# Two groups of v products in a pair of heads instead of three, and the side work placed anew

## The chip, the cores and the metric

The kernel runs on one core of a Trainium2 chip. The metric is the device time of one execution in microseconds (us). A core has five engines that run on their own and meet at semaphores: TensorE (PE) for matmuls, VectorE (DVE), ScalarE (ACT), GpSimd (POOL), and SyncE (SP), whose queue issues most transfers.

## The reference

```
# q, k, v: [4 batches, 8 heads, 768, 64]; centroids: [8 heads, 16, 64]
q_assign = argmax(normed(q) @ normed(centroids).T)        # the same for k
scores   = where(q_assign == k_assign, q @ k.T / 8, -1e9)
attn     = softmax(scores);  x = attn @ v                 # 3072 tokens of 512
skip     = x @ w_skip > 0;   e = argmax(x @ w_gate)       # 8 experts
out      = x + (skip ? gate * relu(x @ w1[e]) @ w2[e] : 0)
```

## The kernel before

Attention comes first, then the experts. Attention works on 16 pairs of heads, one after the other. Queries are taken in two halves of 384 (hf), keys in six tiles of 128 (kt), and the two heads of a pair are a = 0 and 1. So a pair has 24 score tiles, and `score(i, s)` makes one: two matmuls into one bank (the high parts with the mask rows and the maxima as extra rows, L652; the products of high and low parts, L653), `exp` on ScalarE (L655) into one of `NPT` buffers, and GpSimd's running sum of it (L661, L667). `smax` looks ahead for the next pair, 24 times per pair: one matmul of high parts, 128 queries by 384 keys (L603), whose row maxima VectorE takes (L605). `avs` multiplies finished exp tiles with v, in full fp32 and with the two heads in two column halves of the array (L678). It runs in groups of `GROUP` key tiles, both heads of each.

The order of everything is written out by hand. A time is a number of score steps from the pair's first score, 24 steps to a pair, and `steps` issues all steps of all pairs in the order of these times, each on its engine's queue, in order. `PLAN` holds the times of an ordinary pair, `FIRST`, `LAST` and `END` those of the first and last pairs. Negative times lie in earlier pairs: -46.48 is step 1.52 of the pair two before. So the work around a group at step 1.6, 9.6 or 17.6 belongs to several pairs:

- `sims` (L509): similarities of a later pair to the centroids, on TensorE; `assign` finds the nearest centroid on VectorE in seven operations; `masks` makes the mask rows on ScalarE (L566) and sends them in eight transfers (L572).
- `split_hi` (ScalarE, L450) and `split_lo` (VectorE, L460) split q and k; `copies_hi` and `copies_lo` are transfers on SP's queue.
- `mneg` (VectorE, L619) joins the maxima of one half; `mrows` turns them on TensorE (L627), and ScalarE copies them into the score operand (L638) in three pieces.
- `sums` (TensorE, L719) and `recip` (VectorE) make the softmax divisors; `av_out` (ScalarE, L704, L707) takes a group's result out of its bank.
- `xout` turns a half of the output (L780, three turns), scales it on VectorE (`scale_out`, L785) or on ScalarE (`scale_rows`, L802, six copies) and sends it.
- After each batch (four pairs), `route_a` (TensorE, L861), `route_gates` and `route_slots` choose experts, VectorE's steps at the times of `GATES` and `SLOTS`.

Score banks: eight PSUM banks are handed out in turn; a step takes two, one for the scores and one for the maxima.

```
    "av": 1.6, "oT": (0.35, 3.55), "sums": 33.55, ...
        for g in range(n, 2 * KT + 1, n):
            add(2 * g + p["av"], self.avs, keys[g - n:g])
```

With n = 4 the groups of a pair come at 9.6, 17.6 and 25.6, the last of these at step 1.6 of the next pair.

Of the kernel before, what the change touches and what calls it, by code (L numbers as in the profile page):

```python
# [13 lines left out]
F32 = mybir.dt.float32  # L14
# [9 lines left out]
P = 128  # L24
# [4 lines left out]
KT = S // P  # L29
# [19 lines left out]


PLAN = {
    "load": -60.0, "load_v": -45.0, "weights": 72.0, "sims": -46.48, "assign": (-46.42, 0.02, 0.02, 0.02, (-38.42,), 0.02),
    "hi": (-38.405, -38.40), "masks": (-32.5, 0.12), "lo": (-30.38, -22.38), "copies": (-22.1, -21.2, -21.1),
    "smax": (-21.6, 1.0, -0.2), "mneg": (-9.2, 4.0), "mrows": ((-6.5, 0.2, 0.05), (9.62, 0.1, 0.05)),
    "av": 1.6, "oT": (0.35, 3.55), "sums": 33.55, "recip": 33.56, "xout": (33.66, 49.55, 41.55),
    "route": (41.5, 41.55, 65.5), "early": (86.1, 100.9),
}

GATES = (41.62, 41.63, 41.64, 41.65, 41.66, 49.66, 49.67, 49.68, 49.69, 49.7, 57.5, 58.5,
         65.603, 65.604, 65.605, 65.606, 65.607, 65.608, 65.609, 65.61, 65.7)  # L60
SLOTS = ((73.69, 73.7, 73.71, 73.72, 89.65, 97.68, 97.69, 97.7, 97.71, 105.66, 113.66, 117.2, 117.4,
          121.66, 121.67, 121.68, 121.69, 121.7, 121.71, 121.72),
         (73.601, 73.602, 73.603, 73.604, 73.605, 73.606, 73.7, 81.651, 81.652, 81.655, 81.66, 85.0, 85.2,
          86.6, 86.61, 104.4, 104.41, 104.42, 104.43, 104.44))
FIRST = {
    0: {
        "load_v": -18.9, "sims": -20.0, "hi": (-19.9, -19.8, -19.7, -19.6), "assign": (-19.0, 0.1, 0.01, 0.01, 0.01, 0.01),
        "lo": (-18.7, -18.6, -16.9, -16.8), "masks": -17.0, "smax": (-14.0, 0.1, 14.1, 0.7), "mneg": (-12.85, 9.3),
        "mrows": ((-12.8, 0.1, 0.0), (9.65, 0.1, 0.0)),
    },  # L70
    1: {
        "sims": -42.2, "hi": (-42.4, -42.3), "lo": (-40.1, -40.0), "copies": (-20.9, -20.8, -20.7), "load_v": -14.0,
        "assign": (-36.83, 12.93, 0.2, 0.2, 0.2, 0.2), "masks": (-21.6, 0.1), "smax": (-15.6, 0.95, -0.1),
        "mneg": (-4.6, 6.6), "mrows": ((-3.8, 0.2, 0.05), (9.45, 0.1, 0.05)),
    },
    2: {
        "load": -62.0, "load_v": -37.0, "sims": -38.46, "assign": (-38.42, 0.02, 0.02, 0.02, (-30.38,), 0.02), "hi": (-36.2, -30.3), "lo": (-22.39, -22.38), "masks": (-26.0, 0.12), "smax": (-17.6, 0.97, 0.0), "mneg": (-6.4, 5.2),
    },
    3: {"load": -64.0},
    4: {"load": -63.5},  # L80
}

LAST = {"sums": 29.2, "recip": 29.21, "xout": (31.52, 49.55, 37.55)}
END = {"mrows": ((-6.3, 0.2, 0.05), (5.5, 0.1, 0.05)), "mneg": (-9.2, 1.45)}

GROUP = (4, 3)


class Kernel:
# [6 lines left out]
    def run(self):  # L96
        tc = self.tc
        with ExitStack() as ctx:
            self.const = ctx.enter_context(tc.tile_pool(name="const", bufs=1))
            self.raw = ctx.enter_context(tc.tile_pool(name="rawp", bufs=RING))  # L100
            self.halves, self.chosen, self.apart_rows = {}, {}, False

            self.both = ctx.enter_context(tc.tile_pool(name="both", bufs=1))
            self.D = self.both.tile([P, 66 * 256], F32R, name="D")
            self.NPT = 12
            self.PT = self.const.tile([P, self.NPT, HALF + 1], F32, name="PT")
            psum = ctx.enter_context(tc.tile_pool(name="psum", bufs=1, space=PSUM))
# [233 lines left out]
    def tasks(self, i):  # L341

        p, last = {**PLAN, **FIRST.get(i, {}), **({self.npair - 2: LAST, self.npair - 1: END}.get(i, {}))}, i == self.npair - 1
        r = [(s, lambda s=s: self.score(i, s)) for s in range(NS)]
        add = lambda t, f, *a: r.append((t, lambda: f(i, *a)))
        if i:
            add(p["load"], self.load)
        add(p["load_v"], self.load_v)
        if i == 2:
            for a in range(2):  # L350
                add(8.0 + 6.0 * a - i * NS, self.set_rows, a)
        add(p["sims"], self.sims)
# [836 lines left out]
    def ending(self, i):  # L1189

        j = [i // HP * KT + hf * NB for hf in range(2)]
# [13 lines left out]
        for t, c, k in ((25.8, 0, 0), (25.87, 0, 1), (25.94, 0, 2), (25.95, 0, 3), (25.96, 1, 0), (26.05, 1, 1),  # L1205
# [16 lines left out]
    def early_lists(self, i):  # L1222
# [4 lines left out]
        yield (86.3,)  # L1227
# [679 lines left out]
```

## Time and profile before

| | |
|---|---|
| Time, median of 3 runs | 595.55 us (594.94 to 595.74) |
| Profiled execution | 594.91 us, of which the span of the trace is 593.2 us |
| Granted TensorE clock, mean | 0.997 of full speed |

The span runs from the first to the last instruction. Start times in the rows are us from its start. In rows in order of time, the second number is how long the merged instructions lasted, and x is their count. Matmuls overlap: one that lasts 0.34 us may start 0.18 us after another, so starts are compared, not lengths.

### The profile page before, as it was taken

The page shows a single profiled execution, that of the slowest core. Times are in us where ns is not written, and L with a number is a line of the kernel's source. Part 1 is how long each engine was busy: PE and PEld are TensorE (multiplying, and loading weights), DVE is VectorE, ACT ScalarE, POOL GpSimd, SP SyncE. Part 2 cuts the span into 40 slices and gives each one's busy share as a digit, 9 for nine tenths or more (in the row PEclk, how much of TensorE's full clock was granted, in tenths as well). Part 3 has the DMA queues.
Part 4 walks back from the last instruction along what each step waited for, and adds up shares of the span by engine and source line. Part 5 has one row for each costly group of instructions (what it writes and reads, how often), then busy time and mean ns, then how long its engine had stood idle before and what let it go on. Part 6 is the DMA issues. An engine that isn't in the chain of part 4 may idle for free.

```text
span 593.2 us, 12894 instructions
## 1 busy us (share of the span) xinstructions
PE 581.6 (98%) x4225; PEld 419.3 (71%) x4225; DVE 500.6 (84%) x1070; ACT 390.8 (66%) x836; POOL 351.6 (59%) x389
## 2 busy tenths in 40 slices
PE   7999999999999999999999999999999999999996
PEld 3566677767777667776677767775589896677784
DVE  6989897789998989999999999998869863678783
ACT  7466777767777677676777668885336443666572
POOL 7797777867768778577777677784021251243111
PEclk9999999999999999999999999999999999999998
DMA  7378797696876857557576564232344595978860
GB/s 221 85 209 174 183 249 180 189 238 201 231 194 189 201 148 203 141 150 189 152 211 158 135 173 114 75 104 85 110 143 152 206 335 197 362 254 270 268 233 36
DMA packets 53813, 109.00 MB, mean 184 GB/s; under 512 B 8365, under 2 KB 22573, under 8 KB 53744
## 3 DMA queue, kind: packets, MB, share of 16 engines
q1 hardware_dynamic: 51232, 101.92, 60.4%
q0 software_dynamic: 2112, 6.03, 2.9%
q8 instruction: 35, 0.57, 0.4%
q14 instruction: 34, 0.28, 0.2%
q10 hardware_dynamic: 400, 0.20, 0.1%
HBM read 59.95 MB, written 9.57 MB: 117 GB/s over the span
## 4 chain that ended last, share of the span: by engine, by line
PE 86%; issue 5%; DVE 4%; ACT 2%; DMA 1%; POOL 1%; POOLq 0%; SPq 0%; ACTq 0%; DVEq 0%
PE ps L678 22%; PE ps L652 12%; PE ps L603 11%; PE ps L653 11%; PE ps L1095 5%; PE ps L1096 5%; PE ps L1097 5%; PE ps L780 2%; PE ps L719 2%; PE ps L509 2%; PE ps L1690 1%; PE ps L1665 1%; PE ps L627 1%; DMA D<-mk 1%; PE ps L1516 1%
## 5 line engine op out<-in xcount | busy, mean ns | idle before, releaser
L667 POOL TENSOR_TENSOR acc<-acc,PT 128x384 f32<-128x384 f32 x246 | 233.9, 981 | 50.9 <-ACT PT L655 50.7
L605 DVE TENSOR_REDUCE M<-ps 128x1 f32<-128x384 f32 x384 | 197.9, 553 | 16.2 <-PE ps L603 13.4
L655 ACT ACTIVATE PT<-ps 128x384 f32<-128x384 f32 x384 | 177.6, 491 | 35.5 <-PE ps L653 22.6
L652 PE MATMUL ps<-D 102*128 102x384 f32 x384 | 137.2, 357 | 0.0
L678 PE MATMUL ps<-PT,vt 128*64 128x385 f32 x768 | 135.1, 493 | 0.0
L603 PE MATMUL ps<-D 96*128 96x384 f32 x384 | 130.0, 345 | 2.1 <-ACT D L583 1.0
L653 PE MATMUL ps<-D 128*128 128x384 f32 x384 | 130.2, 339 | 0.0
L678 PEld LDWEIGHTS ps<-PT,vt 128*64 128x64 f32 x768 | 50.6, 136 | 61.3 <-issue 56.9
L652 PEld LDWEIGHTS ps<-D 102*128 102x128 f32 x384 | 72.8, 190 | 22.7 <-issue 7.2
L661 POOL TENSOR_TENSOR acc<-PT 128x384 f32<-128x384 f32 x64 | 54.5, 869 | 47.8 <-ACT PT L655 47.7
L603 PEld LDWEIGHTS ps<-D 96*128 96x128 f32 x384 | 73.0, 190 | 5.5 <-ACT D L583 1.4
L653 PEld LDWEIGHTS ps<-D 128*128 128x128 f32 x384 | 73.1, 190 | 0.0
L638 ACT ACTIVATE D<-ps,blocks 6x256 fp32r<-6x256 f32 x84 | 33.2, 456 | 28.0 <-PE ps L627 27.7
L1504 ACT ACTIVATE D<-wraw 128x1024 fp32r<-128x1024 f32 (+1 forms) x45 | 43.2, 997 | 1.4 <-PE ps L1097 1.0
L1509 DVE TENSOR_TENSOR D<-wraw,D 128x1024 fp32r<-128x1024 f32 (+1 forms) x29 | 33.6, 1183 | 6.0 <-ACT D L1504 6.0
L1272 POOL DMA_INDIRECT out<-yo,idws x9 | 11.8, 1314 | 45.2 <-DVE yo L1129 32.4
L460 DVE TENSOR_TENSOR raw<-raw,D 128x768 fp32r<-128x768 f32 x28 | 29.5, 1055 | 0.1
L1272 POOL DMA_INDIRECT out<-PT,idws x4 | 6.5, 1636 | 36.4 <-DVE PT L1701 24.4
L802 ACT ACTIVATE x<-ps,rs 128x64 f32<-128x64 f32 x84 | 18.7, 321 | 11.5 <-PE ps L780 11.5
L1095 PE MATMUL ps<-D 128*128 128x512 f32 x60 | 24.9, 414 | 0.0
L450 ACT ACTIVATE D<-raw 128x768 fp32r<-128x768 f32 x30 | 23.7, 835 | 0.8 <-issue 0.7
L704 ACT ACTIVATE vm<-ps 128x1 f32<-128x1 f32 x31 | 5.3, 172 | 26.1 <-PE ps L678 25.9
(352 smaller groups left out, 943.6 us busy)
## 6 DMA issues: line engine op xcount, KB each, us to landing
wraw<-w SPq DMA_DIRECT2D x72, 512.0 KB, 6.1
D<-D SPq DMA_DIRECT2D x124, 192.0 KB, 3.4
raw<-qk SPq DMA_DIRECT2D x16, 768.0 KB, 5.7
D<-raw SPq DMA_DIRECT2D x60, 192.0 KB, 3.5
vt<-v SPq DMA_DIRECT2D x16, 384.0 KB, 4.1
out<-x SPq DMA_DIRECT2D x31, 192.0 KB, 2.6
D<-mk SPq DMA_DIRECT2D x120, 24.0 KB, 2.0
out<-x ACTq DMA_DIRECT2D x1, 192.0 KB
```

The lines of the kernel that those rows point to most:

```text
L603: nc.tensor.matmul(sm, lhsT=c["qm"][a][0:96, j * P:(j + 1) * P], rhs=c["kb"][a][0:96, hf * HALF:(hf + 1) * HALF], start=True, stop=True)
L605: nc.vector.tensor_reduce(out=c["m"][:, j, a, hf:hf + 1], in_=sm, axis=AX.X, op=ALU.max)
L638: nc.scalar.activation(out=rows[:, :, n0 + b * P:n0 + (b + 1) * P], in_=mp[96:MR, :P].unsqueeze(1).to_broadcast([MR - 96, 2, P]), func=AF. ...
L652: nc.tensor.matmul(ps, lhsT=c["kb"][a][:MR, ks], rhs=c["qm"][a][:MR, sl], start=True, stop=False)
L653: nc.tensor.matmul(ps, lhsT=c["kc"][a][:, ks], rhs=c["qc"][a][:, sl], start=False, stop=True)
L655: nc.scalar.activation(out=pt, in_=ps, func=AF.Exp, scale=D ** -0.5)
L661: nc.gpsimd.tensor_tensor(out=acc, in0=self.pt(i, s - 2)[:, :HALF], in1=pt, op=ALU.add)
L667: (nc.vector if dve else nc.gpsimd).tensor_tensor(out=acc, in0=acc, in1=pt, op=ALU.add)
L678: nc.tensor.matmul(av[a * D:(a + 1) * D, :], lhsT=c["vt"][:, kt, a * D:(a + 1) * D], rhs=self.pt(i, hf * 2 * KT + kt * 2 + a), start=(kt = ...
L1095: mm(ps, lhsT=ah, rhs=bl, start=first, stop=False)
L1504: self.nc.scalar.activation(out=self.W[f"w{w + 1}h"][k][:, cs], in_=self.halves[e, w][k][:, cs], func=AF.Copy)
L1509: self.nc.vector.tensor_tensor(out=self.W[f"w{w + 1}l"][k][:, cs], in0=self.halves[e, w][k][:, cs], in1=self.W[f"w{w + 1}h"][k].bitcast(F3 ...
```

## The change

For pairs 1 to 14 a pair's v products run in two groups of six key tiles (24 matmul instructions) at steps 13.6 and 25.6 (1.6 of the next pair) instead of three groups of four. Pair 0 keeps groups of four, the last pair groups of three. There are 14 exp buffers instead of 12. The output's tile has one buffer instead of two, and the last pair's takes another tile's place.

The side work moves to the two places. The next pair's maxima are spread evenly, one per step from 2 to 25, instead of 2.4 to 13.4 and 14.2 to 25.2. Their turns (`mrows`) come at 13.59 and 1.59, each ahead of a group, instead of 17.5 and 9.62. The sums come at 13.5 instead of 9.55, both halves of the output's turns at 1.55 instead of one at 9.66 and one at 1.55, and both are scaled on ScalarE except in the last three pairs. High parts and masks move to 13.6, the low parts to 13.64 and 1.56, the router's steps as the times show. Pairs 1 and 2 have times of their own: the maxima of pairs 1 and 2 are done earlier, and their turns stand at other steps (pair 2: -6.0 and 6.0, right after its maxima are joined). In the last batch the pieces of the first expert's weights move to step 13.7 of pair 14.

```diff
 PLAN = {
-    "load": -60.0, "load_v": -45.0, "weights": 72.0, "sims": -46.48, "assign": (-46.42, 0.02, 0.02, 0.02, (-38.42,), 0.02),
-    "hi": (-38.405, -38.40), "masks": (-32.5, 0.12), "lo": (-30.38, -22.38), "copies": (-22.1, -21.2, -21.1),
-    "smax": (-21.6, 1.0, -0.2), "mneg": (-9.2, 4.0), "mrows": ((-6.5, 0.2, 0.05), (9.62, 0.1, 0.05)),
-    "av": 1.6, "oT": (0.35, 3.55), "sums": 33.55, "recip": 33.56, "xout": (33.66, 49.55, 41.55),
-    "route": (41.5, 41.55, 65.5), "early": (86.1, 100.9),
+    "load": -60.0, "load_v": -45.0, "weights": 72.0, "sims": -46.48, "assign": (-46.42, 0.02, 0.02, 0.02, (-34.48,), 0.02),
+    "hi": (-34.405, -34.40), "masks": (-34.42, 0.12), "lo": (-34.36, -22.44), "copies": (-22.1, -21.2, -21.1),
+    "smax": ((-22.0, 1.0, 24),), "mneg": (-10.5, 1.5), "mrows": ((-10.41, 0.0, 0.0), (1.59, 0.0, 0.0)),
+    "av": 1.6, "oT": (0.35, 3.55), "sums": 37.5, "recip": 37.56, "xout": (49.55, 49.56, 0.0),
+    "route": (37.51, 37.57, 73.55), "early": (85.52, 100.9),
 }
-GATES = (41.62, 41.63, 41.64, 41.65, 41.66, 49.66, 49.67, 49.68, 49.69, 49.7, 57.5, 58.5,
+GATES = (37.62, 37.63, 37.64, 49.7, 49.71, 49.72, 49.73, 49.74, 49.75, 49.76, 49.77, 51.0,
...
     1: {
-        "assign": (-36.83, 12.93, 0.2, 0.2, 0.2, 0.2), "masks": (-21.6, 0.1), "smax": (-15.6, 0.95, -0.1),
-        "mneg": (-4.6, 6.6), "mrows": ((-3.8, 0.2, 0.05), (9.45, 0.1, 0.05)),
+        "assign": (-36.83, 12.93, 0.2, 0.2, 0.2, 0.2), "masks": (-21.6, 0.1), "smax": ((-15.6, 1.0, 2), (-14.45, 1.0, 1), (-14.0, 1.0, 8), (-6.45, 0.01, 2), (-6.0, 1.0, 8), (1.55, 0.45, 2), (3.0, 1.0, 1)),
+        "mneg": (-6.3, 3.5), "mrows": ((-3.5, 0.2, 0.05), (7.5, 0.1, 0.05)),
...
     2: {
+        "hi": (-36.2, -30.3), "lo": (-30.35, -22.38), "masks": (-26.0, 0.12), "smax": ((-17.6, 1.0, 7), (-10.45, 0.01, 3), (-10.0, 1.0, 12), (1.55, 0.01, 2)),
+        "mneg": (-8.5, 1.57), "mrows": ((-6.0, 0.2, 0.05), (6.0, 0.1, 0.05)),
...
-GROUP = (4, 3)
+GROUP = (4, 6, 3)
...
-            self.NPT = 12
+            self.NPT = 14
...
-        n = GROUP[last]
+        n = GROUP[2 if last else i > 0]
...
-            c["x"] = self.work.tile([P, KT, P], F32, name="x")
+            c["x"] = self.work.tile([P, KT, P], F32, name="x", bufs=1)
...
-        if i >= self.npair - 3 or hf == 0:
+        if i >= self.npair - 3:
             self.scale_out(i, hf, xp)
```

## Rows read from the trace of the kernel before

**Rows 1.** The page's table of engines: busy us (share of the span), instructions.

```profile
PE 581.6 (98%) x4225; PEld 419.3 (71%) x4225; DVE 500.6 (84%) x1070; ACT 390.8 (66%) x836; POOL 351.6 (59%) x389
```

**Rows 2.** Busy time by pair: stretch, length, engines in order PE to POOL, clock, DMA.

```profile
54.41:79.05 24.64, 24.64 (x172) 17.78 (x172) 21.69 (x43) 18.57 (x44) 18.23 (x21) 1.00 0.84 210
...
103.29:127.53 24.24, 24.24 (x170) 17.34 (x169) 20.14 (x40) 18.28 (x44) 18.76 (x21) 1.00 0.81 214
...
127.53:153.37 25.84, 25.84 (x233) 18.65 (x232) 24.01 (x52) 18.27 (x44) 18.04 (x21) 1.00 0.75 212
```

**Rows 3.** TensorE in order of time, one pair: start, length, line, operation, count.

```profile
103.02 0.34 PE L603 MATMUL ps<-D 96*128 96x384 f32 x1
103.29 0.87 PE L719 MATMUL ps<-acc,ones 128*32 128x96 f32 x32
104.09 2.81 PE L678 MATMUL ps<-PT,vt 128*64 128x385 f32 x16
...
106.99 0.49 PE L780 MATMUL ps<-ident,oT 128*128 128x128 f32 x3
...
107.50 0.34 PE L653 MATMUL ps<-D 128*128 128x384 f32 x1
...
108.21 0.33 PE L603 MATMUL ps<-D 96*128 96x384 f32 x1
...
108.71 0.34 PE L653 MATMUL ps<-D 128*128 128x384 f32 x1
...
111.54 0.34 PE L603 MATMUL ps<-D 96*128 96x384 f32 x1
...
111.92 2.81 PE L678 MATMUL ps<-PT,vt 128*64 128x385 f32 x16
...
114.94 0.34 PE L653 MATMUL ps<-D 128*128 128x384 f32 x1
...
118.83 0.34 PE L603 MATMUL ps<-D 96*128 96x384 f32 x1
...
120.35 2.81 PE L678 MATMUL ps<-PT,vt 128*64 128x385 f32 x16
...
123.37 0.34 PE L653 MATMUL ps<-D 128*128 128x384 f32 x1
```

**Rows 4.** TensorE in order of time, a group of the last pair.

```profile
400.33 2.16 PE L678 MATMUL ps<-PT,vt 128*64 128x385 f32 x12
...
402.71 0.34 PE L653 MATMUL ps<-D 128*128 128x384 f32 x1
```

**Rows 5.** TensorE in order of time, turn and group behind the router's block.

```profile
236.58 0.33 PE L627 MATMUL ps<-ident,MX 128*128 128x128 f32 x1
236.84 2.81 PE L678 MATMUL ps<-PT,vt 128*64 128x385 f32 x16
```

**Rows 6.** Waits from 56 to 420 us: total, times, longest.

```profile
PEld ps L652 <- ACT D L638: 2.7, 13, 0.2
```

**Rows 7.** TensorE in order of time, a turn inside a stretch, pair 0.

```profile
41.60 0.34 PE L653 MATMUL ps<-D 128*128 128x384 f32 x1
41.92 0.33 PE L627 MATMUL ps<-ident,MX 128*128 128x128 f32 x1
42.00 0.42 PE L603 MATMUL ps<-D 96*128 96x384 f32 x1
42.26 0.34 PE L652 MATMUL ps<-D 102*128 102x384 f32 x1
```

**Rows 8.** ScalarE in order of time, the same pair as rows 3.

```profile
112.74 1.19 ACT L638 ACTIVATE D<-ps,blocks 6x256 fp32r<-6x256 f32 x3
...
120.46 1.33 ACT L802 ACTIVATE x<-ps,rs 128x64 f32<-128x64 f32 x6 [0.88 <-PE ps L780]
```

**Rows 9.** VectorE in order of time, the same pair.

```profile
115.49 4.26 DVE L605 TENSOR_REDUCE M<-ps 128x1 f32<-128x384 f32 x8 [2.15 <-PE ps L603]
```

**Rows 10.** SP's transfers in order of time, the same pair.

```profile
111.98 5.45 SPq L572 DMA_DIRECT2D D<-mk  x8
```

More of the change, by code (lines that the diff above doesn't have):

```diff
@@ L51 @@
 PLAN = {
-    "load": -60.0, "load_v": -45.0, "weights": 72.0, "sims": -46.48, "assign": (-46.42, 0.02, 0.02, 0.02, (-38.42,), 0.02),
-    "hi": (-38.405, -38.40), "masks": (-32.5, 0.12), "lo": (-30.38, -22.38), "copies": (-22.1, -21.2, -21.1),
-    "smax": (-21.6, 1.0, -0.2), "mneg": (-9.2, 4.0), "mrows": ((-6.5, 0.2, 0.05), (9.62, 0.1, 0.05)),
-    "av": 1.6, "oT": (0.35, 3.55), "sums": 33.55, "recip": 33.56, "xout": (33.66, 49.55, 41.55),
-    "route": (41.5, 41.55, 65.5), "early": (86.1, 100.9),
-}
-GATES = (41.62, 41.63, 41.64, 41.65, 41.66, 49.66, 49.67, 49.68, 49.69, 49.7, 57.5, 58.5,
-         65.603, 65.604, 65.605, 65.606, 65.607, 65.608, 65.609, 65.61, 65.7)
-SLOTS = ((73.69, 73.7, 73.71, 73.72, 89.65, 97.68, 97.69, 97.7, 97.71, 105.66, 113.66, 117.2, 117.4,
+    "load": -60.0, "load_v": -45.0, "weights": 72.0, "sims": -46.48, "assign": (-46.42, 0.02, 0.02, 0.02, (-34.48,), 0.02),
[3 more added lines that the diff above has]
+    "route": (37.51, 37.57, 73.55), "early": (85.52, 100.9),
+}
+GATES = (37.62, 37.63, 37.64, 49.7, 49.71, 49.72, 49.73, 49.74, 49.75, 49.76, 49.77, 51.0,
+         61.65, 61.66, 61.67, 61.68, 73.61, 73.62, 73.63, 73.64, 73.65)
+SLOTS = ((73.69, 73.7, 73.71, 73.72, 85.65, 97.68, 97.69, 97.7, 97.71, 97.72, 109.65, 113.2, 121.6,
           121.66, 121.67, 121.68, 121.69, 121.7, 121.71, 121.72),
-         (73.601, 73.602, 73.603, 73.604, 73.605, 73.606, 73.7, 81.651, 81.652, 81.655, 81.66, 85.0, 85.2,
-          86.6, 86.61, 104.4, 104.41, 104.42, 104.43, 104.44))
+         (73.69, 73.7, 73.71, 73.72, 73.73, 73.74, 73.75, 73.76, 73.77, 73.78, 73.79, 85.51, 85.6,
+          88.6, 88.61, 104.4, 104.41, 104.42, 104.43, 104.44))
 FIRST = {
@@ L67 @@
         "load_v": -18.9, "sims": -20.0, "hi": (-19.9, -19.8, -19.7, -19.6), "assign": (-19.0, 0.1, 0.01, 0.01, 0.01, 0.01),
-        "lo": (-18.7, -18.6, -16.9, -16.8), "masks": -17.0, "smax": (-14.0, 0.1, 14.1, 0.7), "mneg": (-12.85, 9.3),
+        "lo": (-18.7, -18.6, -16.9, -16.8), "masks": -17.0, "smax": ((-14.0, 0.1, 12), (1.3, 0.7, 12)), "mneg": (-12.85, 9.3),
         "mrows": ((-12.8, 0.1, 0.0), (9.65, 0.1, 0.0)),
@@ L72 @@
         "sims": -42.2, "hi": (-42.4, -42.3), "lo": (-40.1, -40.0), "copies": (-20.9, -20.8, -20.7), "load_v": -14.0,
-        "assign": (-36.83, 12.93, 0.2, 0.2, 0.2, 0.2), "masks": (-21.6, 0.1), "smax": (-15.6, 0.95, -0.1),
-        "mneg": (-4.6, 6.6), "mrows": ((-3.8, 0.2, 0.05), (9.45, 0.1, 0.05)),
-    },
-    2: {
-        "load": -62.0, "load_v": -37.0, "sims": -38.46, "assign": (-38.42, 0.02, 0.02, 0.02, (-30.38,), 0.02), "hi": (-36.2, -30.3), "lo": (-22.39, -22.38), "masks": (-26.0, 0.12), "smax": (-17.6, 0.97, 0.0), "mneg": (-6.4, 5.2),
+        "assign": (-36.83, 12.93, 0.2, 0.2, 0.2, 0.2), "masks": (-21.6, 0.1), "smax": ((-15.6, 1.0, 2), (-14.45, 1.0, 1), (-14.0, 1.0, 8), (-6.45, 0.01, 2), (-6.0, 1.0, 8), (1.55, 0.45, 2), (3.0, 1.0, 1)),
+        "mneg": (-6.3, 3.5), "mrows": ((-3.5, 0.2, 0.05), (7.5, 0.1, 0.05)),
+    },
+    2: {
+        "load": -62.0, "load_v": -37.0, "sims": -38.46, "assign": (-38.42, 0.02, 0.02, 0.02, (-30.38,), 0.02),
+        "hi": (-36.2, -30.3), "lo": (-30.35, -22.38), "masks": (-26.0, 0.12), "smax": ((-17.6, 1.0, 7), (-10.45, 0.01, 3), (-10.0, 1.0, 12), (1.55, 0.01, 2)),
+        "mneg": (-8.5, 1.57), "mrows": ((-6.0, 0.2, 0.05), (6.0, 0.1, 0.05)),
     },
@@ L80 @@
     4: {"load": -63.5},
+    6: {"lo": (-22.45, -22.44)},
+    10: {"lo": (-22.45, -22.44)},
+    14: {"lo": (-22.45, -22.44), "mrows": ((-10.41, 0.0, 0.0), (1.75, 0.0, 0.0))},
 }
@@ L366, in tasks @@
             add(p["masks"], self.masks_first)
-        t0, dt, gap, dt2 = (*p["smax"], p["smax"][1])[:4]
-        for n in range(24):
-            add(t0 + dt * n if n < 12 else t0 + 12 * dt + gap + dt2 * (n - 12), self.smax, n)
+        for n, t in enumerate(t0 + dt * j for t0, dt, m in p["smax"] for j in range(m)):
+            add(t, self.smax, n)
         for hf in range(2):
@@ L823, in xout_last @@
         if hf == 0:
-            c["x"] = self.work.tile([P, KT, P], F32, name="x")
+            c["x"] = self.OT[(i + 1) % 5].rearrange("p (j c) -> p j c", c=P)
         xp = self.turn_out(i, hf)
@@ L1212, in ending @@
               (26.57, self.early_second, 4, 7), (26.7, self.rows_last), (26.75, self.early_second, 7, KF)]
-        for w, k, part, t in ((0, 0, 0, -14.35), (0, 1, 0, -14.34), (0, 0, 1, -6.3), (0, 2, 0, -6.2), (0, 3, 0, 1.68),
+        for w, k, part, t in ((0, 0, 0, -10.3), (0, 1, 0, -10.29), (0, 0, 1, -10.2), (0, 2, 0, -10.28), (0, 3, 0, 1.68),
                               (0, 1, 1, 2.2), (0, 2, 1, 6.2), (1, 0, 0, 1.7), (1, 1, 0, 1.72), (0, 3, 1, 9.5),
@@ L1226, in early_lists @@
         nc.tensor.matmul(cp, lhsT=self.ones_bf, rhs=self.cum, start=True, stop=True)
-        yield (86.3,)
+        yield (85.65,)
         pad = self.rt.tile([P, 1], F32, name="pad")
```

## The prediction

> **What bounds the kernel now.** I read the page's engine table first, then the busy time of each pair of heads, then TensorE's instructions in order of time for one undisturbed pair, then the waits.
>
> TensorE is busy for 98% of the span [rows 1]. That alone does not prove a bound, so look at a pair: in 24.24 us TensorE never pauses, VectorE is busy 20.14 us, ScalarE 18.28 us, GpSimd 18.76 us, at full granted clock (1.00, the 2.4 GHz level) [rows 2]. In order of time the pair has three stretches of eight steps (two score matmuls and one maxima matmul each), and between them three clusters of other matmuls around a group of v products [rows 3]. Within a stretch nothing waits: from 114.94 to 118.83 are 22 matmuls in 3.89 us, 0.177 us each, 0.53 us a step. So the pair's time is the sum of TensorE's own starts, and what the change saves or adds there counts in full, while the other engines keep up.
>
> **A cluster's fixed cost.** Count each cluster from the last maxima matmul before it to the second score matmul after it. Around group 9.6 (sums, group, four turns) that is 103.02 to 107.50, 4.48 us; around 17.6 (one turn, group) 111.54 to 114.94, 3.40; around 1.6 (similarities, three turns, group) 118.83 to 123.37, 4.54 [rows 3]. Together 12.42 us. A group of four key tiles takes 3.02 us from its start to that second score matmul (111.92 to 114.94), the last pair's group of three 2.38 [rows 3, 4]: 0.64 per key tile, and 0.46 that comes once per group, of which 0.18 is the score step that any place would have.
>
> **The change, part by part.**
>
> *Two groups of six.* A group of six takes 3.02 + 2 x 0.64 = 4.30 us to the second score matmul. The cluster at 1.6 now has the similarities and three turns as before (118.83 to 120.35, 1.52), plus three more turns of the output and one of the maxima. Three turns last 0.49 us against 0.33 for one, so 0.08 each, 0.32 more [rows 3, 7]. Sum 6.14. The cluster at 13.6 has the sums (103.02 to 104.09, 1.07), the turn of the maxima, and the group. No row has sums, then a turn, then a group; nearest is the router's matmul block, turn, group, where the turn takes 0.26 before the group starts [rows 5]; the bound below is 0.08. I take 0.26: 5.63. Together 11.77, and as one cluster fewer interrupts the steps, two matmul starts (0.35) come back: 12.12 against 12.42. That is 0.30 us for each of the 14 pairs 1 to 14, **4.2 us**; with a turn at 0.08, 6.7.
>
> *The maxima's turn ahead of the second half.* At 9.62 the turn is now made two slots before its rows are used, and score 12 waits for ScalarE's copy: 108.21 to 108.71 are two starts in 0.50 instead of 0.35, **0.15 us**. The waits list the same wait 13 times [rows 6]. In the new plan the copy is made at 1.59, ten steps ahead, so 13 x 0.15 = **1.9 us** goes.
>
> *Lone turns.* Pair 2's two turns, pair 1's second and pair 15's first now stand at 18, 6, 7.5 and 17.7, inside stretches. A lone turn of this kind is at 41.92: 41.60 to 42.26 is 0.66 for two starts (0.35) and the turn (0.08), so 0.23 over, with some wait on VectorE in it; the bound below is the 0.08 by which the start after it is late [rows 7]. I take 0.15, four times: **0.6 us** lost. The Trainium skill (TensorEngine Tiling (Array Packing), Tiling Modes) says that changing the tiling mode drains the engine, and only that; a turn has the same full-array mode as the scores, so by this rule a lone turn would cost nothing and the forecast would be 589.4. The row shows that it does cost something, with no change of tile.
>
> *The output's first half scaled on ScalarE, as the second is.* VectorE loses one scaling per pair; ScalarE gains six copies, which take 1.33 us in a row [rows 8]. Both halves follow the maxima copy (1.19) in the cluster at 1.6. Counted from the cluster's first start (0.27 after the last maxima matmul), the maxima's turn ends near 1.85; ScalarE then works 1.19 + 2 x 1.33 = 3.85 to 5.7, when the group's last result comes too. The second score matmul starts at 6.14 - 0.27 = 5.87 and its result is there at 6.2. So ScalarE is free in time: 0.
>
> *VectorE's side work placed at the clusters.* Eight maxima take 4.26 us, so with one at 0.55 their starts are 0.53 apart, TensorE's own step [rows 9]: a long stretch does not put VectorE behind, but it has no room in one either. All its side work must fit into the clusters. Of 20.14 us some 12.7 are maxima (24 x 0.53), and 0.56 goes: 6.9 remain for 5.4 + 5.9 us of clusters. Cost 0. In the pairs that carry the router VectorE has 3.9 us more (24.01 against 20.14 [rows 2]), and most of the first batch of steps sits at 13.57 to 13.64; with TensorE's router block there too, I make VectorE about 0.4 late at the end of that cluster. Eight banks are four steps, 2.1 us, and a maximum is done 0.92 after its matmul starts (115.49 + 4.26 against 118.83 [rows 3, 9]), so lateness up to about 1 us costs nothing. Cost 0, bound above 1 us for each of three batches.
>
> *Queues.* The high parts' four transfers leave SP at 13.6 instead of 9.6, behind the load, and the eight mask transfers right after them, at 14.0 instead of 15.9. The masks hold the queue 5.45 us [rows 10], and behind them wait the weight load, the copies of the next pair and the output; first needed are the masks, 12 steps and a cluster later (over 12 us). Hidden. GpSimd's sums move nowhere; with 14 exp buffers and 18.8 us of work in about 23.8 it stays under. One output buffer instead of two is written once per pair and sent right after: 0.
>
> *Start and end.* Pair 1's span is 24.64 against 24.24 [rows 2], so the start has 0.4 us of other waits per pair. Its maxima are moved between pairs 0 and 1 and none are removed. I take 0, with 1.5 either way. Two small router blocks of pair 14 join a cluster; not counted.
>
> **Sum.** -4.2 - 1.9 + 0.6 = -5.5 us. The profiled execution took 594.91 us (593.2 of span, 1.7 around it), so 589.4; the median of the runs is 0.64 above it: **590.0 us**.
>
> **Rivals.**
>
> 1. *VectorE crowded in the router's pairs.* Nine of the thirteen pairs carry router steps, now heaped on fewer places. For: 24.01 busy of 25.84. Against: the lateness allowed. Price: 1 us per batch, three batches: 593.0.
> 2. *The maxima's turn waits at 13.6.* It now follows the last maximum closely: ready about 0.92 + 0.1 after the last maxima matmul, while TensorE reaches the turn after 0.27 + 0.80. That just fits. If VectorE ends a stretch 0.4 later than it does there [rows 9], each pair loses 0.4: 13 x 0.4 = 5.2, 595.2, no change.
> 3. *ScalarE late after the cluster at 1.6* (the other side). If twelve copies cost their own 0.32 each (3.9 instead of 2.7), ScalarE starts the exps some 1.2 - 0.3 = 0.9 late and, with the copy of the group's result behind them, about 1.1. If half of that reaches TensorE through the score banks, 13 x 0.6 = 7.8 is lost: 597.8, slower. It decides from 0.42 us a pair. Against: six copies in 1.33 in the row itself.
> 4. *The start gains too*: two more exp buffers and earlier masks for pairs 1 and 2 take away waits there: 1.5 us more, 588.5.
>
> That the change does not do what it says is excluded where the fixed cost is concerned: it shows on both sizes of group [rows 3, 4].
>
> **Chances.** Forecast 0.62, rival 1 0.17, rival 2 0.06, rival 3 0.08, rival 4 0.07. About 0.2% (1.2 us) is what a measurement can tell from no change. Faster 0.62 + 0.17 + 0.07 = 0.86, same 0.06, slower 0.08. The range goes from a turn at 0.08 with part of the start's gain (588.2) to rival 1 with a little more (593.6); rivals 2 and 3 are left out.
>
> **What would show it.** Right: groups of 24 instructions near 4.1 us, two per pair; undisturbed pairs of about 23.8 us; no wait of a score for the maxima's copy; ScalarE idle before the first exp after the cluster at 1.6. Wrong: a gap before the maxima's turn at 13.6 (rival 2), score starts farther apart than 0.177 early in a stretch (rival 3) or in router pairs alone (rival 1).

## The result, and the profile after

The changed kernel is slower: 603.39 us (median of 4 runs, 602.0 to 603.48) against 595.39 (594.94 to 595.74) for the kernel before; the ratio is 1.0129, 95% interval 1.0112 to 1.0147. I forecast 590.0 and gave "slower" 8 in 100. In the changed kernel lines 403 and up carry numbers higher by 4 (a score's first matmul is L656, its second L657, a maxima matmul L607, the maximum L609, v products L682).

The page's head: a span of 601.7 us instead of 593.2, with TensorE at 97% and VectorE at 85%, as in [rows 1] within a point.

```profile
PE 582.6 (97%) x4225; PEld 425.1 (71%) x4225; DVE 511.5 (85%) x1057; ACT 410.6 (68%) x914; POOL 361.3 (60%) x389
```

So the loss is no engine's load. First an undisturbed pair: the windows give pair 6, counted from the second score matmul behind one group at 1.6 to that behind the next, 24.06 us where [rows 2] have 24.24.

```profile
174.69:198.75 24.06, 24.00 (x169) 17.59 (x169) 23.08 (x47) 19.84 (x50) 19.08 (x20) 1.00 0.77 204
```

TensorE's order of time in the same pair, the two clusters, to be read as [rows 3]: last maxima matmul, what stands ahead of the group, the group, the second score matmul behind it.

```profile
180.71 0.34 PE L607 MATMUL ps<-D 96*128 96x384 f32 x1
180.97 0.87 PE L723 MATMUL ps<-acc,ones 128*32 128x96 f32 x32
181.90 0.33 PE L631 MATMUL ps<-ident,MX 128*128 128x128 f32 x1
182.16 4.10 PE L682 MATMUL ps<-PT,vt 128*64 128x385 f32 x24
186.48 0.34 PE L657 MATMUL ps<-D 128*128 128x384 f32 x1
...
192.49 0.33 PE L607 MATMUL ps<-D 96*128 96x384 f32 x1
192.75 0.85 PE L513 MATMUL ps<-raw,cb 128*32 128x384 f32 x8
193.53 0.87 PE L784 MATMUL ps<-ident,oT 128*128 128x128 f32 x6
194.24 0.27 PE L631 MATMUL ps<-ident,MX 128*128 128x128 f32 x1
194.45 4.10 PE L682 MATMUL ps<-PT,vt 128*64 128x385 f32 x24
...
198.76 0.34 PE L657 MATMUL ps<-D 128*128 128x384 f32 x1
```

The cluster at 13.6 takes 180.71 to 186.48, 5.77 us (forecast 5.63), the one at 1.6 takes 192.49 to 198.76, 6.27 (6.14). With the 0.35 of one cluster fewer that is 12.39 against 12.42, a gain of 0.03 and not 0.30; the wait of score 12 [rows 6] is gone, 0.15. Together that is the 0.18 that the pair shows. Not every pair shows the same: counted from one group at 1.6 to the next, pairs 2, 3, 6, 7, 10 and 11 are 0.17 to 0.27 shorter than before, and pairs 4 and 12, which carry the router's matmul block, 0.59 and 0.58 (25.26 and 25.25 us against 25.85 and 25.83). What gives these two their 0.6 is not taken apart here. The eight together are 2.3 us shorter.

What outweighs it is in the waits from 56 to 420 us: a new row, five scores waiting for a bank that VectorE's maximum still holds.

```profile
PE ps L656 <- DVE M L609: 7.1, 5, 1.6
```

The five stand behind the group at 1.6 in pairs 5, 8, 9, 13 and 14 (152, 226, 254, 355 and 380 us). Here is the third: VectorE in order of time, from the joining of the maxima taken ahead of the group (L623).

```profile
244.49 0.17 DVE L623 TENSOR_REDUCE MX<-M 128x6 f32<-128x18 f32 x1
244.60 3.53 DVE L464 TENSOR_TENSOR raw<-raw,D 128x768 fp32r<-128x768 f32 x2
248.05 0.57 DVE L546 STREAM_TRANSPOSE ss<-ps 128x384 f32<-128x384 f32 x1
...
251.27 0.52 DVE L540 TENSOR_TENSOR ohe<-wts,mwe 128x48 f32<-128x48 f32 x1
251.82 0.79 DVE L942 SCALAR_TENSOR_TENSOR ohd<-L,ohe 128x48 bf16<-128x48 f32 x1
...
252.94 2.92 DVE L609 TENSOR_REDUCE M<-ps 128x1 f32<-128x384 f32 x6
```

From 244.49 to 252.94 VectorE does side work: 8.45 us, while the undisturbed cluster lasts 6.27. In the kernel before, the same place held 4.4 us of it, from the first row here to the second:

```profile
244.94 0.58 DVE L542 STREAM_TRANSPOSE ss<-ps 128x384 f32<-128x384 f32 x1 [0.25 <-PE ps L509]
...
249.30 1.01 DVE L605 TENSOR_REDUCE M<-ps 128x1 f32<-128x384 f32 x2
```

The table of times sets both low parts of pairs 6, 10 and 14 at 1.55 and 1.56 of the pair ahead (their lines are in the diff of "Low parts back" below); the kernel before had one of the two here. In pair 9 they take 3.53. Beside them GpSimd, in order of time, runs eight sums without a break:

```profile
240.23 8.63 POOL L671 TENSOR_TENSOR acc<-acc,PT 128x384 f32<-128x384 f32 x8
```

TensorE in order of time and the windows of 2 us behind the gap (the column ahead of the last two is the granted clock):

```profile
253.54 0.44 PE L656 MATMUL ps<-D 102*128 102x384 f32 x1 [1.64 <-DVE M L609]
...
254.74 0.52 PE L607 MATMUL ps<-D 96*128 96x384 f32 x1
255.06 0.52 PE L656 MATMUL ps<-D 102*128 102x384 f32 x1
```

```profile
254.00:256.00 2.00, 2.00 (x8) 2.00 (x8) 1.86 (x4) 1.40 (x4) 2.00 (x3) 0.56 0.77 230
256.00:258.00 2.00, 2.00 (x8) 2.00 (x8) 1.12 (x2) 1.07 (x3) 2.00 (x3) 0.58 0.64 206
```

Behind this gap the granted clock falls to 0.56 and 0.58 in the two windows, most of them at the 1.2 GHz level, and matmuls start 0.32 us apart instead of 0.177; the twelve starts from 254.18 to 257.82 lose 1.5 us. The same follows the gap at 379.83; the other three gaps are followed by a clock of 1.00. That is 7.1 us of idle time and 3.0 at the lower clock. Counted by starts the loss is larger: from group to group the five pairs take 25.86, 26.66, 27.63, 24.86 and 27.21 us, and in the kernel without sums (the first experiment) 24.23, 25.26, 24.24, 23.26 and 23.87, 11.4 less together; the latter are 1.5 below the kernel before. The sum: 11.4 - 1.5 - 2.3 (the eight pairs above) + 0.65 at the start (pair 0's last group ends at 49.48, before at 48.83) + 0.3 behind pair 14 make some 8.5, as much as the spans differ by. (Pair 1 gains 1.28, and the last group of pair 14 is 1.29 longer: these two cancel.)

In pair 8 there is one low part, and it alone takes 3.65 us, where one with no sum beside it takes 0.96. GpSimd's row of ten sums beside it ends at 220.76, and the low part 0.8 us later:

```profile
217.92 3.65 DVE L464 TENSOR_TENSOR raw<-raw,D 128x768 fp32r<-128x768 f32 x1
```

Last the mean durations, VectorE by line and shape, 60 to 405 us (operations, mean ns of one):

```profile
L609 DVE TENSOR_REDUCE M<-ps 128x1 f32<-128x384 f32 x328 | 171.6, 555 | 17.7 <-PE ps L607 17.3
L464 DVE TENSOR_TENSOR raw<-raw,D 128x768 fp32r<-128x768 f32 x26 | 32.4, 1255 | 0.0
L540 DVE TENSOR_TENSOR oh<-wts,mwc 128x384 bf16<-128x384 f32 x12 | 12.1, 1004 | 0.4
```

The same view of the kernel before:

```profile
L605 DVE TENSOR_REDUCE M<-ps 128x1 f32<-128x384 f32 x331 | 171.3, 554 | 14.0 <-PE ps L603 11.5 <-ACT PT L655 1.9
L460 DVE TENSOR_TENSOR raw<-raw,D 128x768 fp32r<-128x768 f32 x26 | 27.1, 1042 | 0.1
L536 DVE TENSOR_TENSOR oh<-wts,mwc 128x384 bf16<-128x384 f32 x12 | 7.6, 629 | 0.4
```

The maxima, which read PSUM, are as they were; the same operations with both inputs in SBUF became longer. That gave two suspects: the heap of side work, and GpSimd's sums getting in the way of it.

### The profile page after: what moved, and what is told of

Read it like the earlier page. It is cut to its first block, busy times and chain, and to the rows that moved or that the text cites. A ratio compares the mean times of both kernels' runs of the same rounds, so it can differ in the third digit from the quotient of the medians.

```text
span 601.7 us, 12930 instructions
## 1 busy us (share of the span) xinstructions
PE 582.6 (97%) x4225; PEld 425.1 (71%) x4225; DVE 511.5 (85%) x1057; ACT 410.6 (68%) x914; POOL 361.3 (60%) x389
## 4 chain that ended last, share of the span: by engine, by line
PE 69%; DVE 21%; issue 4%; ACT 2%; DMA 2%; POOL 1%; ACTq 0%; POOLq 0%; DVEq 0%
PE ps L682 18%; DVE M L609 12%; PE ps L656 9%; PE ps L607 7%; PE ps L657 7%; PE ps L1099 5%; PE ps L1100 5%; PE ps L1101 5%; PE ps L513 2%; PE ps L784 2%; DVE raw L464 2%; PE ps L1694 1%; DMA wraw<-w 1%; PE ps L1669 1%; PE ps L1520 1%
## 5 line engine op out<-in xcount | busy, mean ns | idle before, releaser
L671 POOL TENSOR_TENSOR acc<-acc,PT 128x384 f32<-128x384 f32 x246 | 240.2, 1011 | 8.5 <-ACT PT L659 8.3
L609 DVE TENSOR_REDUCE M<-ps 128x1 f32<-128x384 f32 x384 | 199.6, 554 | 19.8 <-PE ps L607 18.9
L659 ACT ACTIVATE PT<-ps 128x384 f32<-128x384 f32 x384 | 180.3, 494 | 29.4 <-PE ps L657 19.4
L656 PE MATMUL ps<-D 102*128 102x384 f32 x384 | 137.3, 358 | 7.2 <-DVE M L609 7.1
L607 PE MATMUL ps<-D 96*128 96x384 f32 x384 | 131.8, 349 | 1.6 <-ACT D L587 1.0
L682 PE MATMUL ps<-PT,vt 128*64 128x385 f32 x768 | 132.0, 491 | 0.0
L657 PE MATMUL ps<-D 128*128 128x384 f32 x384 | 131.5, 342 | 0.0
L665 POOL TENSOR_TENSOR acc<-PT 128x384 f32<-128x384 f32 x64 | 56.1, 895 | 88.0 <-ACT PT L659 88.0
L682 PEld LDWEIGHTS ps<-PT,vt 128*64 128x64 f32 x768 | 52.0, 136 | 62.4 <-issue 60.2
L656 PEld LDWEIGHTS ps<-D 102*128 102x128 f32 x384 | 73.7, 192 | 30.8 <-issue 16.8
L607 PEld LDWEIGHTS ps<-D 96*128 96x128 f32 x384 | 73.8, 193 | 5.9 <-ACT PT L659 1.8
L657 PEld LDWEIGHTS ps<-D 128*128 128x128 f32 x384 | 74.0, 193 | 0.0
L464 DVE TENSOR_TENSOR raw<-raw,D 128x768 fp32r<-128x768 f32 x28 | 34.7, 1247 | 0.0
L806 ACT ACTIVATE x<-ps,rs 128x64 f32<-128x64 f32 x156 | 33.4, 345 | 1.3 <-PE ps L784 0.9
```

The source lines that it names most:

```text
L464: eng.tensor_tensor(out=lo.bitcast(F32R), in0=lo, in1=c[f"hi{t}"].bitcast(F32), op=ALU.subtract)
L607: nc.tensor.matmul(sm, lhsT=c["qm"][a][0:96, j * P:(j + 1) * P], rhs=c["kb"][a][0:96, hf * HALF:(hf + 1) * HALF], start=True, stop=True)
L609: nc.vector.tensor_reduce(out=c["m"][:, j, a, hf:hf + 1], in_=sm, axis=AX.X, op=ALU.max)
L656: nc.tensor.matmul(ps, lhsT=c["kb"][a][:MR, ks], rhs=c["qm"][a][:MR, sl], start=True, stop=False)
L657: nc.tensor.matmul(ps, lhsT=c["kc"][a][:, ks], rhs=c["qc"][a][:, sl], start=False, stop=True)
L659: nc.scalar.activation(out=pt, in_=ps, func=AF.Exp, scale=D ** -0.5)
```

## The experiments

**No sums.** In the changed kernel, sums are left out from the third key tile on:

```diff
-elif kt > 1 and not (i == self.npair - 1 and hf and kt >= KT - 2):
+elif kt > 1 and i == self.npair - 1 and not (hf and kt >= KT - 2):
```

> The changed kernel without GpSimd's running sums from the third key tile on, in all pairs but the last (so the softmax divisors are too small); GpSimd keeps 4 of 20 additions per pair. If VectorE's side operations are long because GpSimd's additions hold the SBUF path that both use, then the operations with two inputs from SBUF go back (low parts from 1255 ns mean to about 950, the one-hot compare from 1004 to about 570, the two before it from 791 and 761 to about 560), the five gaps of TensorE behind a maximum (7.1 us) and the two slow stretches behind them (2.9 us) go, and the time is about 593.5; pairs without router steps stay at 24.06. Rival, simply too many operations at two places: the durations hardly move, the gaps stay above 1 us, 601 to 603.

Measured: 593.01 us (591.53 to 599.05), ratio 0.9977 (0.9952 to 1.0003). No score waits for VectorE's maxima, and the operations are short (the same view):

```profile
L464 DVE TENSOR_TENSOR raw<-raw,D 128x768 fp32r<-128x768 f32 x26 | 24.6, 954 | 0.0
L540 DVE TENSOR_TENSOR oh<-wts,mwc 128x384 bf16<-128x384 f32 x12 | 6.7, 558 | 0.4
```

The heap of pair 9, the same operations in the same order, is over in 5.87 us instead of 8.45 (from 241.85 to the second row here):

```profile
241.96 1.83 DVE L464 TENSOR_TENSOR raw<-raw,D 128x768 fp32r<-128x768 f32 x2
...
247.72 4.80 DVE L609 TENSOR_REDUCE M<-ps 128x1 f32<-128x384 f32 x9
```

With all of the side work in its heaps the loss is gone once the sums are.

**Low parts back.**

```diff
-    6: {"lo": (-22.45, -22.44)},
-    10: {"lo": (-22.45, -22.44)},
-    14: {"lo": (-22.45, -22.44), "mrows": ((-10.41, 0.0, 0.0), (1.75, 0.0, 0.0))},
+    14: {"mrows": ((-10.41, 0.0, 0.0), (1.75, 0.0, 0.0))},
```

> The changed kernel with the low parts of pairs 6, 10 and 14 at their ordinary places (13.64 and 1.56), so that one of the two leaves the cluster at step 1.6 in which eight router steps are done. If VectorE's lateness makes the gaps, the three gaps behind those clusters (1.37, 1.64 and 1.34 us) and one slow stretch (1.4) go: 597.5 to 599.5. Rival, the router's exp on ScalarE holds the score exps behind it: it still waits for VectorE's last router step, gaps of 1 us stay, 602 or more. A third way: the low part makes the cluster at 13.6 of pairs 4, 8 and 12 late instead, a gap there of 0.5 to 1 us each.

Measured: 596.43 (594.58 to 602.36), ratio 1.0051 (1.0018 to 1.0084). Four of the five gaps are gone from the trace, one of 1.48 at 372.85 (pair 14) is left:

```profile
PE ps L654 <- DVE M L607: 1.5, 1, 1.5
```

The heap is the other half of the cause. Two reservations: the trace is of an execution of 594.85, so it does not show what the longer ones (up to 602.36) waited for. And pair 8's heap was not touched, yet its gap is gone: its low part took 1.87 us this time and not 3.65. That one is not the edit's doing.

**Router's exp later.**

```diff
-GATES = (..., 49.77, 51.0,
+GATES = (..., 49.77, 55.0,
```

> The changed kernel with the router's exp on ScalarE four steps later (at step 7 instead of 3 behind the cluster), so that the score exps no longer stand behind one that waits for VectorE. If the maxima hold the banks, the gaps stay as they are: 603.4, within 0.6. Rival, ScalarE's in-order wait makes them: three gaps shrink by a us or more, and 599 to 601 results.

Measured: 607.56 (606.51 to 608.89), ratio 1.022 (1.0199 to 1.0241), 4 us longer where one expectation had no change and the other a gain. ScalarE's waiting was not the cause. The gaps of pairs 5, 9 and 13 grow, to 2.16, 3.02 and 2.15 (why stays open), and that of pair 8 is gone:

```profile
PE ps L656 <- DVE M L609: 8.8, 4, 3.0
```

**The maxima's turn behind the group at 13.6** (the same for pair 14, which has its own line).

```diff
-    "mrows": ((-10.41, 0.0, 0.0), ...
+    "mrows": ((-10.39, 0.0, 0.0), ...
```

> The changed kernel with the turn of the maxima for the first half issued right behind the group at 13.6 instead of between the sums and the group. If what the clean pair lost against the forecast is TensorE's cost of a turn between sums and group (0.92 us from sums to turn where the sums alone lead to the group in 0.80, then 0.26 more), each pair gains about 0.3: 13 x 0.3 = 4, so 599.5. Rival: ScalarE's three copies now stand before the first score exps of the stretch and hold them, the gain is given back: 602.5 to 603.5.

Measured: 621.52 (620.42 to 623.73), ratio 1.0441 (1.0419 to 1.0463). Neither theory had this: in nearly every pair a maxima matmul now waits until ScalarE has emptied the group's bank, by the code because a bank is taken in the order in which the banks came back (take and give); that reading is not tested apart.

```profile
PE ps L607 <- ACT oT L711: 10.6, 12, 0.9
PE ps L656 <- DVE M L609: 10.2, 6, 3.5
```

It tells nothing of the turn's own price. Of the two places, ahead of the group is the better one.

**Router steps of pair 14 parted** (on top of "low parts back").

```diff
-(73.69, ..., 73.74, 73.75, 73.76, 73.77, 73.78, 73.79, 85.51, 85.6,
+(73.69, ..., 73.74, 73.75, 81.651, 81.652, 81.655, 81.66, 85.51, 85.6,
```

> The changed kernel with the low parts of pairs 6, 10 and 14 at their ordinary places (as in the run before) and, besides, the second batch's router steps of pair 14 parted: the one-hots' last part, the ranks' sums and the weighted rows (four steps) go 8 key tiles later, as they stand in the kernel before, the other seven stay behind the group at 1.6. My theory (TensorE's gaps come where VectorE has more side work behind one group than the maxima's banks give it time for): the last gap of the run before, 1.48 us in pair 14, falls away, no gap of more than 0.5 us at a score is left, and the time is 1 to 2 us below the 596.4 of that run: 594.4 to 595.4, the kernel before within its measurement. Rival (the gap moves: the four steps find the maxima just as short of time 8 key tiles later): a gap of 1 us or more near 378 us, 596.4.

Measured: 601.19 (596.17 to 602.65), ratio 1.0102 (1.0071 to 1.0133): worse than both expectations. The gap that the rival expected near 378 us is there (1.43 at 377.72, at a router matmul), and a larger one came up. The trace has the clearest single line of the study; VectorE, GpSimd and TensorE in order of time:

```profile
384.60 5.63 DVE L1049 TENSOR_TENSOR cc<-ohd,ecode 128x48 f32<-128x48 bf16 x1
```

```profile
383.83 1.98 POOL L663 TENSOR_TENSOR acc<-PT 128x384 f32<-128x384 f32 x2
385.76 4.40 POOL L669 TENSOR_TENSOR acc<-acc,PT 128x384 f32<-128x384 f32 x5
```

```profile
390.99 0.67 PE L605 MATMUL ps<-D 96*128 96x384 f32 x1 [4.62 <-DVE M L607]
```

A product of 48 elements a partition (its like takes 0.18 to 0.20 in the other batches of this trace and in the kernel before) came into a row of seven sums, the last of which ended at 390.16, and ended itself 0.07 us later. TensorE waited 4.62 us, and the clock was at 0.66 in the 5 us behind.

**The kernel before, without sums** (same edit as in the first run).

> The kernel before with GpSimd's running sums left out from the third key tile of each half on in all pairs but the last (the output differs): the same cut as in the run that left them out of the changed kernel, 593.0 us. It tells what the grouping alone is worth on TensorE where no sum stands in VectorE's way. Theory (each pair gains 0.18 us in its groups and the score's wait of 0.15 us goes, so 14 x 0.18 + 1 or 2 us of waits, partly lost at the start): before without sums stays at 594.5 to 595.5, since its TensorE waited for VectorE nowhere in the middle pairs, and the changed one without sums is 1.5 to 2.5 us below it. Rival (the sums cost the kernel before just as much, and the grouping is worth nothing): before without sums falls to about 593, level with the changed one. If the grouping were worth the full 5.5 us that I forecast, this run would come out near 598, which nothing in its trace supports.

Measured: 594.18 (593.88 to 595.14) beside 594.24, ratio 0.9999 (0.999 to 1.0008). The sums cost the kernel before nothing. Without sums the changed kernel's median is 1.9 us below its own kernel before, this one's 0.1. I put that difference down to the grouping; the first run's interval (to 1.0003) just reaches no change, so by itself it does not show it.

**GpSimd held behind the side work.** The sums of the fifth and sixth key tile of a half are written behind the side steps, and the first of them waits for the newest of VectorE's operations (`self.vec` is VectorE):

```diff
+            held = 0 < i < self.npair - 1 and kt >= 4
+            if held:
+                yield ((25.99 if hf else 13.79) + 0.0001 * s,)
+                side = [u for u in list(nc.cur_bb.bb.instructions) if u.engine == self.vec][-1]
             (nc.vector if dve else nc.gpsimd).tensor_tensor(out=acc, in0=acc, in1=pt, op=ALU.add)
+            if held and (kt, a) == (4, 0):
+                self.tc.add_manual_dep(self.newest(), side.name, mybir.DependencyInfo(
+                    mybir.DependencyClass.Sync, mybir.DependencyReason.DATA), reason="pause")
```

> The changed kernel, and in it GpSimd is made to stand still behind each group of six's start: in pairs 1 to 14 the sum of the fifth key tile (first head) of a half waits for the last of VectorE's side operations behind that group, and the half's last three sums stay queued behind it. All sums are still made, later by the stretch that GpSimd was idle behind the group anyway (2.3 to 3.2 us). Theory (VectorE's operations with two inputs in SBUF can't start while GpSimd's sums run back to back; with groups of six GpSimd's idle stretch fell from inside the group to behind it): the low parts come down from 1255 ns to at most 1000 on the mean, eqc, its product, oh and ohd to about 570, the five gaps at the scores shrink to a sum below 1.5 us, and the time falls from 603.4 to 593 to 595.5, all but the whole loss with all of the change's placing kept. Rival (the side work is heaped too high, whatever GpSimd does): the operations get shorter but three or more gaps of over 1 us stay, 599 or more. Second rival (the held sums free the exponentials' slots too late and ScalarE stops): new waits of scores for ScalarE, 603 or more.

Measured: 598.57 (597.14 to 600.49), ratio 1.0069 (1.0049 to 1.0088): half of the loss is back, not all. The gaps at scores shrink from 7.1 to 1.4 us, but not in the way that I expected. The low parts were to come down to 1000 ns at most and became longer (1255 without the hold), and the one-hot compare went from 1004 to 1298:

```profile
L465 DVE TENSOR_TENSOR raw<-raw,D 128x768 fp32r<-128x768 f32 x26 | 35.9, 1388 | 0.0
```

So the hold moved the meetings more than it ended them. And at the end of pair 14 the sums bunch, where VectorE and GpSimd, in order of time, show the wait again:

```profile
392.78 9.32 DVE L1103 TENSOR_TENSOR rawW<-wraw,D 128x1024 fp32r<-128x1024 f32 x1
```

```profile
391.22 7.18 POOL L676 TENSOR_TENSOR acc<-acc,PT 128x384 f32<-128x384 f32 x8
398.37 1.68 POOL L666 TENSOR_TENSOR acc<-PT 128x384 f32<-128x384 f32 x2
400.01 1.00 POOL L676 TENSOR_TENSOR acc<-acc,PT 128x384 f32<-128x384 f32 x1
```

The weights' operation (1.16 us the next time) ends 1.1 us after the row of sums has ended (thirteen since 389.28, of which the last eleven stand here), and the last pair's score waits 1.81 us, for VectorE's next operation.

**Held sums with the low parts back.**

> The same held sums in the kernel that has the low parts of pairs 6, 10 and 14 at their ordinary places (596.4 without the hold, its runs between 594.6 and 602.4). Theory: the last gap (1.48 us in pair 14) goes and with it the spread between executions; 592.5 to 594, 1.5 us or so below the kernel before and near the 593.0 of the changed kernel without sums: the version that beats both. Rival (the grouping alone is worth nothing, and only the sums' absence shortened that run): 595, level with the kernel before.

Measured: 596.91 (594.75 to 598.96), ratio 1.0035 (1.0021 to 1.005): no better than without the hold. The last pair's wait (1.73) and one gap in pair 14 (1.31) are there.

**Held, but not in the last half of pair 14**, alone and with both other edits.

```diff
-            held = 0 < i < self.npair - 1 and kt >= 4
+            held = 0 < i < self.npair - 1 - hf and kt >= 4
```

> The changed kernel with GpSimd's sums held behind VectorE's side work (598.6 in the run before), but not in the last half of pair 14. There the hold ran GpSimd's sums together with the last pair's: a weights' operation of VectorE with two inputs took 9.32 us instead of some 1.2, and the last pair's score waited 1.81 us, the row sums 0.40. Theory: these two waits go and one or two short gaps at the scores stay, 596.0 to 597.0; of the change's loss of 8 us, 6 us or more then come from operations of VectorE kept out by GpSimd's sums. Rival (that operation is late in any case): 598 or more.

> The same hold (but for the last half of pair 14) in the kernel with the low parts of pairs 6, 10 and 14 at their ordinary places, and with the four router steps of pair 14 8 key tiles later. Theory: no gap of over 0.5 us at a score of pairs 1 to 15; 593 to 594.5, below the kernel before by the 1 to 2 us that the grouping showed without sums. Rival (holding costs as much as it frees, or the gain without sums was the missing work's): 595 or more, level with the kernel before or behind it.

Measured: 597.62 (596.49 to 600.32), ratio 1.0049 (1.0031 to 1.0066), and 596.12 (594.76 to 597.72), ratio 1.0029 (1.0015 to 1.0044). Both missed: the last pair's wait stays at 1.80. The row of thirteen sums is there as before, and beside it the weights' operation takes 9.30 and 9.17 us; so it was not the hold in that half that made the row.

**Three gate steps earlier** (on top of "low parts back"; nothing held), and the same with sums held in pairs 1 to 13.

```diff
-         61.65, 61.66, 61.67, 61.68, 73.61, 73.62, 73.63, 73.64, 73.65)
+         61.65, 61.66, 61.67, 61.68, 61.69, 61.7, 61.71, 73.64, 73.65)
```

> The kernel with the low parts of pairs 6, 10 and 14 at their ordinary places (596.4, its last gap 1.48 us in pair 14), and three of the router's five last gate steps 12 key tiles earlier, behind the group at 13.6 of the pair before; nothing held on GpSimd. Theory: the heap behind the group at 1.6 of pairs 6, 10 and 14 loses some 2 us and the last gap goes: 594 to 595.5, level with the kernel before (594.3 to 595.4 on its chips); the executions still spread over some us, since which operation meets a run of sums is a matter of some tenths of a microsecond. Rival (the gap moves to the group at 13.6): 597 or more.

> The same with GpSimd's sums held behind VectorE's side work in pairs 1 to 13 only; in pair 14 the held sums stood in GpSimd's queue before the first gather of rows, and the last pair's score waited 1.80 us for what comes of it, with the hold in its first half alone as with both. Theory: that wait goes too, no score of pairs 1 to 15 waits over 0.5 us, 593 to 594.5, and the executions lie within 2 us of each other: the version that beats both by what the grouping is worth on TensorE. Rival (the wait of the last pair is the last pair's own): 595 to 596.5.

Measured: without the hold 592.59 (591.3 to 594.0), ratio **0.9953** (0.9938 to 0.9969), better than both kernels and than I expected; with it 594.38 (593.41 to 594.91, and one execution of 3190.53), ratio 0.9989 (0.9979 to 0.9999). The place shown above, now in the version without the hold, VectorE in order of time:

```profile
243.47 0.95 DVE L462 TENSOR_TENSOR raw<-raw,D 128x768 fp32r<-128x768 f32 x1
...
249.44 1.01 DVE L607 TENSOR_REDUCE M<-ps 128x1 f32<-128x384 f32 x2
```

The side work is over 6.06 us after the joining of the maxima started (243.38) instead of 8.45, the cluster covers it, and the scores' waits for VectorE shrink to one:

```profile
PE ps L654 <- DVE M L607: 1.2, 1, 1.2
```

It is pair 8's, at 225.35: the heap there was left as it was, and its low part takes 3.65 us again. The low parts still take 1171 ns on the mean here: the sums do not have to go if no heap is too high for them. The hold costs 1.8 us in this version; the last pair's wait is 1.25 with the hold (the weights' operation 8.51 us beside thirteen sums) and is not there without it (3.50 beside ten).

## Why the prediction was wrong

The step that failed is *VectorE's side work placed at the clusters*: "Cost 0, bound above 1 us for each of three batches". I added up VectorE's busy time and set it against the clusters' total, with durations of the kernel before. Two things broke that. The work is not spread evenly: behind the group at 1.6 of pairs 5, 9 and 13 the change puts eight of the router's steps (before five), the assignment and both low parts (before one), so one cluster has to hold what the sum gave to two; in pair 8 it puts eight router steps, the assignment and a low part, in pair 14 sixteen router steps. And the durations did not stay: an operation with two inputs in SBUF can wait when it comes into a row of GpSimd's sums. Before the change a row there had at most six sums, and it ended 2.6 us after the cluster at 1.6 began (118.83 to 121.42); after it ten sums follow each other and end 5.0 us after it began (192.49 to 197.46). GpSimd in order of time, before and then after:

```profile
116.01 5.41 POOL L667 TENSOR_TENSOR acc<-acc,PT 128x384 f32<-128x384 f32 x6 [0.98 <-ACT PT L655]
```

```profile
187.55 1.69 POOL L665 TENSOR_TENSOR acc<-PT 128x384 f32<-128x384 f32 x2 [2.66 <-ACT PT L659]
189.20 8.25 POOL L671 TENSOR_TENSOR acc<-acc,PT 128x384 f32<-128x384 f32 x8
```

So the prediction's "GpSimd's sums move nowhere" did not hold in the trace. The 8.45 us of pair 9 are both things at once: 5.87 that the heap takes without sums, and 2.6 that the sums add. Neither alone costs anything that can be seen in the time: without sums the heaps cost nothing (593.0), without heaps the sums cost nothing (592.6), and in the kernel before the sums cost nothing (0.9999). Together they make the difference between 8.0 us above the kernel before and 2.4 below it, 10.4 us.

The Trainium skill (SBUF — State Buffer, Who interferes with whom and Summary: rules for kernel authors) states this conflict: a VectorE instruction with two inputs in SBUF contends with a GpSimd instruction that reads SBUF, and the one that comes second is blocked for the whole of the other's instruction. The traces agree for the operations with two inputs in SBUF. They differ on how long: 5.63, 9.32 and 3.65 us are waits for whole rows of sums, not for one of some 1.0 us. And two kinds of operation with a single input in SBUF became longer beside a row of sums as well: the divisors' TENSOR_SCALAR (L736) takes 0.17 us alone and 0.60 in a row, the gates' CAST (L976) 0.18 and up to 0.97. The signs were there in the kernel before: its low parts took 0.94 to 1.45 us, and one operation on the weights, with two inputs in SBUF, 3.26 where others took 1.22.

*Two groups of six*: the mechanism was right, the size was not, 0.03 a pair for 0.30. A group of 24 lasts 4.10 as forecast. Seven turns behind the similarities take 0.92 (193.53 to 194.45), where I had 0.81, and the turn at 13.6 stands 0.93 behind the sums' start, where I had 0.80: its weight load waits for VectorE's reduction of the maxima (3.1 us in ten places of the waits), rival 2's place at a third of rival 2's price. With this term right the sum would have been 14 x 0.03 + 1.9 - 0.6 = 1.7 us of gain, 593.8; the version without the heaps of pairs 5, 9 and 13 gains 2.4. The range's lower end, 588.2, does not follow from its own terms: a turn at 0.08 alone, with none of the start's gain, gives 590.0 - 2.5 = 587.5.

*The maxima's turn ahead of the second half*: right, the wait is gone from the list and the pairs show its 0.15. *ScalarE's six more copies* and *queues*: no matmul waits for either from 56 to 420 us of the changed kernel, cost 0 as forecast. *Start*: 0.65 lost, inside its 1.5. *Lone turns*: right, near the 0.15 that I took and not nothing. At 64.40 and at 77.11 the second matmul start behind a lone turn comes 0.47 us after the last one ahead of it instead of 0.35, so a turn costs 0.12.

Rival 1 named the place (router pairs, VectorE) and mis-sized it: 1 us a batch, where the first batch has two gaps (1.4 and 1.2), the second one (1.6) and the third two (1.3 and 1.5), and two of the five are followed by 1.5 us each at the lower clock, which no term of mine contained. By the lengths of the pairs the three batches lost 3.0, 3.4 and 4.9 us. Rival 3 (ScalarE late) fell.

Open is why one operation that meets a row of sums waits 0 to 0.9 us (most of them) and another until the row is over. The low part of pair 8, at the same place, took 3.65, 1.87 and again 3.65 us in the changed kernel, "low parts back" and the best version. It looks like a matter of tenths of a microsecond, and it would fit the spread between executions (594.6 to 602.4 for "low parts back"), but no run settles it. Why holding the sums of earlier halves makes the row at the end of pair 14 thirteen long, on which the last pair's wait follows, is open too.

## What to carry to other kernels

A cluster that is to hide another engine's side work is checked one by one, the fullest first; a sum over the pair hides the heap that decides. And a duration from the kernel before holds only while the same neighbour is beside it: ask of each VectorE operation that reads SBUF, above all with two inputs there, what GpSimd is doing in its new place. When a regrouping that saves a little comes out slower, look for the one place where the work was heaped before giving up the grouping: two small moves turned 1.3% lost into 0.5% gained.

## What the runs showed of the hardware

A VectorE operation of 0.2 us took 5.63, one of 1.2 took 9.32 and one of 0.95 took 3.65, while GpSimd's sums followed each other without a break; they ended 0.07, 1.1 and 0.8 us after the row did. And a TensorE gap of about 1.5 us can cost twice its length: after two of the five (1.64 and 1.51) the clock was granted at the 1.2 GHz level for some 3.6 us, after the other three (1.37, 1.20, 1.34) it was not.
